# Loading weights and later chunks through eight row blocks with gaps, in a delta-rule attention and MoE kernel

## The chip, the cores and the metric

The kernel runs on one core of one Trainium2 chip. The metric is the device time of one execution in microseconds (us), taken as the median of several runs.

## What is computed

Two stages follow each other. The first is a delta-rule recurrence over 768 time steps for 4 x 8 heads of width 48; the second is a gated feed-forward layer (two products, multiplied, then a third) on the 3072 resulting rows.

```python
k_n = k / (np.linalg.norm(k, axis=-1, keepdims=True) + 1e-06)
for t in range(S):
    y[:, :, t] = einsum('bhd,bhde->bhe', q[:, :, t], state)
    v_old = einsum('bhde,bhd->bhe', state, kt)
    state = state + bt * einsum('bhd,bhe->bhde', kt, vt - v_old)
...
a = x @ w_a          # 384 -> 1536
b = x @ w_b
return a * b @ w_out # 1536 -> 384
```

The weights arrive as 64-bit floats, the rest as 32-bit floats.

## The kernel before

**Tiling.** The 768 steps are cut into 24 chunks of 32 (`NCH`), in six groups of four. For a group, `prep` squares keys and values for norms and multiplies the transposed keys and queries of each chunk with each other (`gram_mm`, 128 small matmuls of 32x64 for a whole group in sets of 32); `solve` inverts the triangular systems of the group on VectorE (DVE); `steps` walks its chunks in order, updates the state in PSUM (`S_ps`) and writes the chunk's result, transposed and split into two fp16 parts, to `xb`. Chunks share their input tiles in pairs: `kb` holds natural keys, `vnb` values, `rawb` transposed keys and queries, and `late` is one large tile that serves as weight staging, as one more place for those inputs, and as output buffer.

**Weights.** There are 12 weight blocks, each 1152 KB (128 rows of 1152 float64). `weights(p)` loads one into a slot (two slots in `late`, one in `wh`), unpacks it to float32 on DVE with one TENSOR_SCALAR and two SCALAR_TENSOR_TENSOR of 128x1152, takes its norm (ScalarE, ACT, square with a sum, then a matmul with `ones`), and splits it into a high and a low part (`wh`, `wo`). For the first four blocks the low part goes through TensorE (PE: `zit`, `neg1`, `negr` matmuls).

**MoE.** `moe` does for a pair of chunks and one weight block 18 fp16 matmuls of 128x256, two PSUM evacuations and 6 matmuls of 128x384. These make up most of the PE work (2592 and 864 matmuls).

**Loads.** All loads and stores are issued on SyncE's queue (SP) by `load` (line 690 and on). Some are held back by tiny GpSimd (POOL) copies into the target that read an earlier target (the list `NEXT`, and `prep` for groups 2 and up), so that a load starts when an earlier one has landed. The host pads rows of weights and of `kqt` by 64 bytes, so that each of 128 rows gives four pieces.

**The order.** Nothing is issued where it is written. The code records operations in `Plan`; `Plan.order` runs a list scheduler over the whole program (`pack`, 6 passes with changing priorities) and `Plan.issue` (line 471) writes the instructions per engine in the order found. `pack` has its own prices: 475 ns of SP time for a load plus bytes/400 ns of transfer (`op.move`), and in `fetch` a price for fetching PE's instructions. There PE's stream is cut into blocks of 256 words (two words for a matmul, four in fp32), a next block is asked for when the one before it is entered, and it comes 3500 ns later, or 5600 ns later while a load is under way by the plan (`LOADED`). An operation that would run out of fetched words is put off in favour of another. Where PE would wait in the first 60 us of the plan, `issue` puts in filler matmuls of `ones` (line 477, 128x256 fp32; they have no reader), up to `SHY` = 1500 ns before the awaited operation. An engine executes its instructions in the order written, so any change of a price can move all that comes after.

Of the kernel before, what the change touches and what calls it, by code (L numbers as in the profile page):

```python
# [15 lines left out]
I32 = mybir.dt.int32  # L16
# [10 lines left out]
P = 128  # L27
# [3 lines left out]
NFC = FF // P  # L31
# [29 lines left out]
class Plan:  # L61
# [131 lines left out]
    def add(self, eng, fn, name, args, kw):  # L193
        isap = lambda a: isinstance(a, bass.AP)
        outs = [a for a in args[:1]] + [kw[k] for k in ("accum_out",) if k in kw]
        ins = [a for a in list(args[1:]) + [v for k, v in kw.items() if k != "accum_out"] if hasattr(a, "tensor")]
        if self.open is not None and self.open and self.open[-1].eng == eng:
            op = self.open[-1]
        else:
            op = Op(eng)  # L200
            kind = self.stream + ("_pe" if self.stream == "moe" and eng == "PE" else "")
            op.pri = len(self.ops) - URGENCY.get(kind, URGENCY.get(kind.rstrip("0123456789"), 0))
            op.deps, self.behind = self.behind, set()
            self.ops.append(op)
            op.tag, op.stream = name, self.stream
            if self.open is not None:
                self.open.append(op)
        op.calls.append((fn, args, kw, dict(self.lease)))
        if eng == "SP":
            op.dur = 475.0  # L210
            n = mybir.dt.size(outs[0].dtype)
            for d in outs[0].shape:
                n *= d
            op.move = max(n / 400.0, 20.0)
        else:
            dur = self.price(eng, name, outs, ins, kw)
            op.dur += dur
            if eng == "PE":
                n = 1
                for d in outs[0].shape[1:]:  # L220
                    n *= d
                k, m, f = ins[0].shape[0] / 128, ins[0].shape[-1] / 128, ins[0].dtype == F32
                op.use += (1 + 3 * f) * n / 2.4 * m * (k + 1) / 2 + 5 * f
                op.words += 4 if ins[0].dtype == F32 else 2
                if min(ins[0].shape[0], ins[0].shape[-1]) <= 64:
                    if len(op.calls) == 1:
                        op.dur += self.SWITCH
                    op.cold += 2 * dur
                else:
                    op.cold += max(outs[0].shape[-1] if len(outs[0].shape) == 2 else 64, 48) / 1.2 * (4 if ins[0].dtype == F32 else 1)  # L230
        for regs, aps in ((op.wr, outs), (op.rd, ins)):
            for a in aps:
                g = self.region(a)
                if g is not None:
                    k = g[:3]
                    n = self.leased(a)
                    if n is not None:
                        op.banks.add(n)
                        k = (n,) + k[1:]
                    regs[k] = regs.get(k, 0) | g[3]  # L240
# [169 lines left out]
        return at, stop, done, max(stop), ({b: h[0] for b, h in held.items()}, fill)  # L410

    MOVE = (1200.0, 1300.0)
    LOADED = (3500.0, 5600.0)
    BEGIN, IDLE, SINCE, UNTIL = 63, (50.0, 440.0), 1200.0, 60e3
    SHY, KEEP, GAIN, HEAT = 1500.0, 0.41, 0.42, (3.0, 430.0)

    def fetch(self, t, n, took, pos, come, dma):
        slip, come, known = 0.0, come[:], len(come)
# [68 lines left out]


@with_exitstack
def tile_kernel(ctx, tc, kqt, kn, vn, begin, w, out):  # L490
    nc = tc.nc
    plan = Plan(nc)
    V, A, T, G, SP = (
        plan.engine(e, o)
        for e, o in (("DVE", nc.vector), ("ACT", nc.scalar), ("PE", nc.tensor), ("POOL", nc.gpsimd), ("SP", nc.sync))
    )
# [35 lines left out]
    WB = 2 * (6 * P + DM)  # L532
# [4 lines left out]
    slots = [late[:, 0:WB], late[:, WB : 2 * WB], whf[:, 3 * WB : 4 * WB]]  # L537
# [17 lines left out]
    def rawp(c):  # L555
        s = SLOT[c // 2]
        return rawb[:, 2 * s : 2 * s + 2] if s < 3 else lf[:, 0:2048].rearrange("p (c d) -> p c d", c=2)

    def knp(c):
        s = SLOT[c // 2]  # L560
        return knb[:, 2 * s : 2 * s + 2] if s < 3 else lf[:, 4352:5120].rearrange("p (c d) -> p c d", c=2)

    def vnp(c):
        s = SLOT[c // 2]
        return vnb[:, 2 * s : 2 * s + 2] if s < 3 else lf[:, 2816:3584].rearrange("p (c d) -> p c d", c=2)
# [117 lines left out]

    loaded, whole = set(), set()

    def target(c, what):
        t = {"w": lambda: slots[c].bitcast(F32), "k": lambda: knp(c)[:, 0], "v": lambda: vnp(c)[:, 0], "r": lambda: rawp(c)[:, 0], "r0": lambda: rawp(c)[:, 0], "r1": lambda: rawp(c)[:, 1]}
        return t[what]()[0:1, 0:1]

    def load(c, what):  # L690
        if (c, what) in loaded:
            return
        loaded.add((c, what))
        if what == "w":
            SP.dma_start(slots[c].rearrange("p (n d) -> p n d", n=4), w[c].bitcast(I32)[:, :, 0 : WB // 4])
        elif what == "k" and c == 0:
            SP.dma_start(kb[:, 0 : begin.shape[1]], begin)
        elif what == "k":
            SP.dma_start(knp(c).rearrange("p c d -> p (c d)"), kn[c // 2])
        elif what == "v":  # L700
            SP.dma_start(vnp(c).rearrange("p c d -> p (c d)"), vn[c // 2])
        elif what == "r":
            SP.dma_start(rawp(c).rearrange("p c (h d) -> p (c h) d", h=2), kqt[c // 2][:, :, 0:512])
        else:
            i = int(what[1])
            loaded.add((c, "r"))
            SP.dma_start(rawp(c)[:, i].rearrange("p (h d) -> p h d", h=2), kqt[c // 2][:, 2 * i : 2 * i + 2, 0:512])

    grams, rest = {}, []

# [40 lines left out]
    def prep(g):  # L751
        chs = GROUPS[g]
        ss = sst
        if g > 1:
            last = []
            for c in chs[2], chs[0]:
                for part in "k", "r0", "r1", "v":
                    if (c, part[0]) in loaded and part != "r1":
                        continue
                    if last:  # L760
                        G.tensor_copy(target(c, part), target(*last))
                    load(c, part)
                    last = c, part
# [426 lines left out]
def _layout(inputs):  # L1190
    f = lambda x: np.ascontiguousarray(x)
    q, k, v = (np.asarray(inputs[n]) for n in ("q", "k", "v"))
    beta = np.asarray(inputs["beta"])

    def tr(x):
        return x.reshape(B, 2, 2, 2, NCH, C, D)

    kq = np.stack([tr(k), tr(q)], axis=4)
    kq[:, :, :, 1] = kq[:, :, :, 1, ::-1].copy()
    kqt = kq.transpose(5, 3, 7, 0, 1, 2, 4, 6).reshape(NCH // 2, 2, 2, D, 1024).transpose(0, 2, 3, 1, 4)  # L1200
    gaps = np.zeros((NCH // 2, 2, 64, 2048), np.float32)
    gaps[:, :, 0:D] = kqt.reshape(NCH // 2, 2, D, 2048)
    pieces = np.zeros((NCH // 2, P, 4, 512 + 16), np.float32)
    pieces[..., 0:512] = gaps.reshape(NCH // 2, P, 4, 512)

    def natl(x):

        return x.reshape(B, 2, 4, NCH, C, D).transpose(3, 2, 4, 0, 1, 5).reshape(NCH // 2, 2, P, 384).transpose(0, 2, 1, 3).reshape(NCH // 2, P, 768)

    bn = beta.reshape(B, 2, 4, NCH, C).transpose(2, 4, 3, 0, 1).reshape(P, NCH, 8)  # L1210
    bp = np.zeros((P, NG, 4, 8), np.float32)
    for g, chs in enumerate(GROUPS):
        for i, c in enumerate(chs):
            bp[:, g, i] = bn[:, c]
    perm = np.empty(DM, np.int64)
    for j in range(3):
        for hp in range(4):
            for e in range(32):
                cc = j * 32 + e
                perm[j * 128 + hp * 32 + e] = ((cc // D) * 4 + (hp ^ 1)) * D + cc % D  # L1220

    masks = np.zeros((P, 32 + P + 2), np.float32)
    masks[:, 0:32] = np.tile(np.triu(np.ones((32, 32), np.float32), 1), (4, 1))
    masks[:, 32 : 32 + P] = np.eye(P, dtype=np.float32)
    masks[:, 32 + P :] = [[1 - p // 32 % 2, p // 32 % 2] for p in range(P)]
    wab = np.stack([np.asarray(inputs["moe_w_a"])[perm], np.asarray(inputs["moe_w_b"])[perm]])
    wab = wab.reshape(2, 3, P, NFC, P).transpose(3, 2, 0, 1, 4).reshape(NFC, P, 6 * P)
    w = np.concatenate([wab, np.asarray(inputs["moe_w_out"]).reshape(NFC, P, DM)], axis=2)
    wide = np.zeros((NFC, P, 4, 288 + 8), w.dtype)
    wide[..., 0:288] = w.reshape(NFC, P, 4, 288)  # L1230
    nat = f(natl(k))
    return {
        "kqt": pieces,
        "kn": nat,
        "vn": f(natl(v)),
        "first": f(np.concatenate([bp.reshape(P, NG * 32), masks, nat[0]], axis=1)),
        "w": wide.view(np.int64),
    }


# [15 lines left out]
```

## Time and profile before

| what | value |
|---|---|
| median of 3 runs | 656.53 us (655.1 to 660.78) |
| the profiled execution: its time | 658.43 us |
| its span, first to last instruction | 656.6 us, so 1.8 us lie around it |
| PE matmul busy | 625.9 us (95%) |
| DVE, ACT, POOL busy | 404.8, 270.4, 25.7 us |
| mean granted PE clock | 0.961 of full speed |
| DMA traffic | 42.78 MB, mean 65 GB/s |
| instruction packets, queue q8 | 95, 1.56 MB |
| weight load, issue to landing | 6.8 us median of the ten into `late` |

All instructions but the fillers carry one line, L486, since one statement issues them; groups are told apart by tiles. PE stands for matmuls, PEld for the weight load into the array that precedes each. A row of the timeline gives start, duration, engine, line, operation and in brackets the idle time before it with what ended it. "issue" there means that the engine waited for nothing that the profile records. PEclk is the granted share of PE's full clock; the DMA column is the busy share of the 16 DMA engines.

### The profile page before, as it was taken

How to read it: one execution, taken by the hardware profiler on the slowest of the kernel's cores; microseconds unless marked ns; L12 is line 12 of the kernel's file. 1: busy time of each engine (PE TensorE's matmuls, PEld its weight loads, DVE VectorE, ACT ScalarE, POOL GpSimd, SP SyncE). 2: the span in 40 equal slices, each digit the busy share in tenths (PEclk: the TensorE clock that was granted, in tenths of full speed). 3: DMA queues.
4: the chain of work that ended last, by engine and by line, in shares of the span. 5: the costliest groups of instructions: out<-in, count | busy, mean ns of one | idle time of the engine just before them, and what ended most of it. 6: DMA issues, size and time to landing. Idle time of an engine off the chain costs nothing.

```text
span 656.6 us, 26617 instructions
## 1 busy us (share of the span) xinstructions
PE 625.9 (95%) x12184; PEld 535.3 (82%) x12184; DVE 404.8 (62%) x1059; ACT 270.4 (41%) x599; POOL 25.7 (4%) x62
## 2 busy tenths in 40 slices
PE   7788999998999999999999999999999999999997
PEld 6575688777788887888878888888888888888887
DVE  5796699768666995448965389754686533222222
ACT  4245684245445634323373234733324333232322
POOL 0000000000012200000020000200000000000000
PEclk8858799879999999999999999999999999999999
DMA  7837202212276000004300033000000000000000
GB/s 252 312 130 272 80 4 74 80 70 76 70 226 190 19 2 27 4 14 134 108 2 29 4 115 112 26 4 28 3 1 26 4 3 25 1 25 2 25 1 24
DMA packets 19824, 42.78 MB, mean 65 GB/s; under 512 B 1280, under 2 KB 4352, under 8 KB 19712
## 3 DMA queue, kind: packets, MB, share of 16 engines
q1 hardware_dynamic: 19712, 41.08, 18.9%
q8 instruction: 95, 1.56, 1.0%
q14 instruction: 17, 0.14, 0.1%
HBM read 36.36 MB, written 4.72 MB: 63 GB/s over the span
## 4 chain that ended last, share of the span: by engine, by line
PE 78%; DVE 12%; ACT 4%; issue 3%; ACTq 0%
PE bank L486 75%; DVE b L486 3%; PE S_ps L486 3%; DVE tmp L486 2%; ACT sqf L486 2%; DVE wh L486 1%; DVE ghl L486 1%; DVE late L486 1%; DVE g L486 1%; ACT ghl L486 1%; ACT tt L486 1%; ACT a L486 0%; DVE sc L486 0%; DVE ss L486 0%; DVE s L486 0%
## 5 line engine op out<-in xcount | busy, mean ns | idle before, releaser
L486 PEld LDWEIGHTS <-wh 128*128 128x128 f16 x2592 | 241.2, 98 | 50.6 <-issue 22.4
L486 PE MATMUL bank<-xb,wh 128*128 128x256 f16 x2160 | 259.8, 273 | 2.2 <-issue 2.2
L486 PE MATMUL bank<-wo,ghl 128*128 128x384 f32 x864 | 192.3, 356 | 0.6 <-issue 0.6
L486 PEld LDWEIGHTS bank<-wo,ghl 128*128 128x128 f32 x864 | 145.2, 190 | 4.8 <-issue 1.6
L486 ACT COPY a<-bank 128x256 f32<-128x256 f32 x144 | 53.6, 372 | 195.4 <-PE bank L486 195.3
L486 DVE TENSOR_TENSOR g<-bank,a 128x256 f32<-128x256 f32 x144 | 60.8, 422 | 114.8 <-ACT a L486 113.5
L486 DVE TENSOR_TENSOR ghl<-g,ghl 128x256 fp32r<-128x256 f32 x144 | 62.3, 432 | 35.0 <-ACT ghl L486 33.8
L486 ACT CAST ghl<-g 128x256 fp32r<-128x256 f32 x144 | 58.1, 404 | 60.4 <-DVE g L486 59.6
L486 PE MATMUL bank<-late,wh 128*128 128x256 f16 x432 | 52.0, 273 | 1.2 <-ACT u L486 1.2
L486 DVE TENSOR_TENSOR b<-b,tmp 128x31 f32<-128x31 f32 (+20 forms) x154 | 50.9, 330 | 2.8
L486 DVE TENSOR_TENSOR tmp<-b,b 128x31 f32<-128x31 f32 (+20 forms) x154 | 50.8, 330 | 2.9
L486 ACT ACTIVATE y<-bank,sc 128x384 f32<-128x384 f32 x24 | 14.0, 582 | 45.1 <-PE bank L486 42.8
L486 DVE SCALAR_TENSOR_TENSOR y<-bank,sc,y 128x384 f32<-128x384 f32 x23 | 14.2, 616 | 29.6 <-ACT y L486 29.6
L486 PEld LDWEIGHTS bank<-rawb 48*32 48x32 f32 x1280 | 21.2, 117 | 7.7 <-issue 3.7
L486 PE MATMUL bank<-rawb 48*32 48x64 f32 x1280 | 24.0, 232 | 3.3 <-DMA rawb<-in_kqt 3.3
L486 DVE TENSOR_TENSOR b<-bank,dc 128x256 f32<-128x256 f32 x24 | 14.5, 605 | 20.6 <-PE bank L486 17.1
L486 PEld LDWEIGHTS bank<-sh,rawb 48*64 48x64 f32 x1216 | 21.3, 144 | 6.7 <-issue 5.3
L486 PEld LDWEIGHTS bank<-f,tt 32*32 32x32 f32 x1472 | 17.9, 107 | 9.3 <-issue 5.5
L486 PE MATMUL bank<-sh,rawb 48*64 48x48 f32 x1216 | 23.9, 229 | 0.7 <-issue 0.7
L486 PE MATMUL bank<-u,at 32*32 32x48 f32 x1536 | 22.3, 206 | 1.9 <-issue 1.9
L486 PE MATMUL bank<-f,tt 32*32 32x48 f32 x1472 | 21.2, 206 | 2.5 <-issue 1.4
L486 DVE TENSOR_TENSOR f<-vnb,bank 128x384 f32<-128x384 f32 x38 | 19.9, 548 | 5.7 <-PE bank L486 5.1
(120 smaller groups left out, 552.8 us busy)
## 6 DMA issues: line engine op xcount, KB each, us to landing
late<-in_w SPq DMA_DIRECT2D x10, 1152.0 KB, 6.8
rawb<-in_kqt SPq DMA_DIRECT2D x12, 512.0 KB, 3.7
out<-late SPq DMA_DIRECT2D x24, 192.0 KB, 1.9
rawb<-in_kqt SPq DMA_DIRECT2D x4, 1024.0 KB, 7.0
vnb<-in_vn SPq DMA_DIRECT2D x10, 384.0 KB, 3.2
kb<-in_kn SPq DMA_DIRECT2D x9, 384.0 KB, 3.9
wh<-in_w SPq DMA_DIRECT2D x2, 1152.0 KB, 9.7
late<-in_kqt SPq DMA_DIRECT2D x4, 512.0 KB, 3.7
```

The costliest lines, as they stand in the source:

```text
L486: fn(*(self.place(a, lease) for a in args), **{k: self.place(a, lease) for k, a in kw.items()})
```

## The change

`load` no longer reads 128 rows. The host cuts each array into 8 blocks of 16 rows, with 2048 bytes of padding behind each block, and `eight` builds a source pattern whose outermost dimension is 8 (block), then 16 or 64 pieces within the block, then the piece. The bytes moved and their places in SBUF are as before. This holds for the 12 weight blocks and for keys, values and `kqt` of chunk 4 and on; the first two pairs of chunks have arrays of their own (`kqt0`, `kn0`, `vn0`) that are read by 128 rows as before. The two halves `r0` and `r1` of a `kqt` load become one load of 1024 KB, which makes eight loads and eight gates fewer. The planner's prices change with it: 200 bytes per ns for loads of eight rows, 3700 ns in place of 5600 for a fetch beside a load, and fillers up to 500 ns before the awaited operation.

```diff
-            op.move = max(n / 400.0, 20.0)
+            op.move = max(n / (200.0 if ins[0].shape[0] == 8 else 400.0), 20.0)
...
-    LOADED = (3500.0, 5600.0)
+    LOADED = (3500.0, 3700.0)
...
-    SHY, KEEP, GAIN, HEAT = 1500.0, 0.41, 0.42, (3.0, 430.0)
+    SHY, KEEP, GAIN, HEAT = 500.0, 0.41, 0.42, (3.0, 430.0)
...
+    def eight(src, n, d):
+        return bass.AP(src.tensor, src.offset, [[src.shape[1], 8], [(src.shape[1] - 512) // n, n], [1, d]])
...
-            SP.dma_start(slots[c].rearrange("p (n d) -> p n d", n=4), w[c].bitcast(I32)[:, :, 0 : WB // 4])
+            SP.dma_start(slots[c].rearrange("p (n d) -> p n d", n=4), eight(w[c].bitcast(I32), 64, WB // 4))
...
-            SP.dma_start(knp(c).rearrange("p c d -> p (c d)"), kn[c // 2])
+            SP.dma_start(knp(c).rearrange("p c d -> p (c d)"), kn0[c // 2] if c < 4 else eight(kn[c // 2], 16, 768))
...
-            SP.dma_start(vnp(c).rearrange("p c d -> p (c d)"), vn[c // 2])
+            SP.dma_start(vnp(c).rearrange("p c d -> p (c d)"), vn0[c // 2] if c < 4 else eight(vn[c // 2], 16, 768))
...
-            SP.dma_start(rawp(c).rearrange("p c (h d) -> p (c h) d", h=2), kqt[c // 2][:, :, 0:512])
-        else:
-            i = int(what[1])
-            loaded.add((c, "r"))
-            SP.dma_start(rawp(c)[:, i].rearrange("p (h d) -> p h d", h=2), kqt[c // 2][:, 2 * i : 2 * i + 2, 0:512])
+            SP.dma_start(rawp(c).rearrange("p c (h d) -> p (c h) d", h=2), kqt0[c // 2][:, :, 0:512] if c < 4 else eight(kqt[c // 2], 64, 512))
...
-                for part in "k", "r0", "r1", "v":
-                    if (c, part[0]) in loaded and part != "r1":
+                for part in "k", "r", "v":
+                    if (c, part) in loaded:
...
+    def blocks(x):
+        x = x.reshape(len(x), 8, -1)
+        return f(np.concatenate([x, np.zeros((len(x), 8, 2048 // x.itemsize), x.dtype)], axis=2))
```

Since the prices change, the order of nearly the whole program changes. Two places matter below. The first is ScalarE's order in the first 21 us. The four `tt` rows copy the four Gram results of the first group out of PSUM; the `sqf` rows are squares of values and of `rawb` for norms.

```order
 L486 COPY tt_86<-bank_62 128x256
 L486 ACTIVATE sqf,sc_127<-vnb 128x768
-L486 ACTIVATE sqf,sc_127<-rawb 48x1024
 L486 COPY tt_87<-bank_63 128x256
-L486 ACTIVATE sqf,sc_127<-rawb 48x1024
-L486 ACTIVATE sqf,sc_127<-vnb 128x768
 L486 ACTIVATE sqf,sc_127<-rawb 48x1024
 L486 COPY tt_88<-bank_64 128x256
 L486 ACTIVATE sqf,sc_127<-rawb 48x1024
+L486 ACTIVATE sqf,sc_127<-vnb 128x768
+L486 ACTIVATE sqf,sc_127<-rawb 48x1024 x2
```

The third copy now has one square ahead of it instead of two, and the fourth has two instead of five; three squares moved behind the fourth copy.

The second place is the head of PE's order: fillers (`ones`), the first group's Gram matmuls (`rawb`, 32 for a chunk), then the first matmuls that need the solved systems (`b_3_71`).

```order
-L477 MATMUL bank_66<-ones 128x256 x6
+L477 MATMUL bank_66<-ones 128x256 x7
 L486 MATMUL bank_61<-rawb 32x64 x32
 L486 MATMUL bank_62<-rawb 32x64 x32
+L477 MATMUL bank_66<-ones 128x256
 L486 MATMUL bank_63<-rawb 32x64 x32
 L486 MATMUL bank_64<-rawb 32x64 x32
-L477 MATMUL bank_66<-ones 128x256 x20
+L477 MATMUL bank_66<-ones 128x256 x26
 L486 MATMUL bank_65<-b_3_71,tt_85 32x16 x32
 L486 MATMUL bank_61<-b_3_71,tt_86 32x16 x32
```

There are 34 fillers instead of 26: one more ahead of the first Gram, one between the second and the third, six more behind the fourth.

More of the change, by code (lines that the diff above doesn't have):

```diff
@@ L489, in tile_kernel @@
 @with_exitstack
-def tile_kernel(ctx, tc, kqt, kn, vn, begin, w, out):
+def tile_kernel(ctx, tc, kqt0, kn0, vn0, begin, kqt, kn, vn, w, out):
     nc = tc.nc
@@ L1230, in _layout @@
     wide[..., 0:288] = w.reshape(NFC, P, 4, 288)
-    nat = f(natl(k))
+    nat, vat = natl(k), natl(v)
+    def blocks(x):
+        x = x.reshape(len(x), 8, -1)
+        return f(np.concatenate([x, np.zeros((len(x), 8, 2048 // x.itemsize), x.dtype)], axis=2))
     return {
-        "kqt": pieces,
-        "kn": nat,
-        "vn": f(natl(v)),
+        "kqt0": f(pieces[0:2]),
+        "kn0": f(nat[0:2]),
+        "vn0": f(vat[0:2]),
         "first": f(np.concatenate([bp.reshape(P, NG * 32), masks, nat[0]], axis=1)),
-        "w": wide.view(np.int64),
+        "kqt": blocks(pieces),
+        "kn": blocks(nat),
+        "vn": blocks(vat),
+        "w": blocks(wide.view(np.int64).reshape(NFC, P, -1)),
     }
```

## The prediction

> **What bounds the kernel now.** I read the page first, then the waits of PE, then the stretches around PE's longest waits, and last the chain of the first 48 us.
>
> ```profile
> PE 625.9 (95%) x12184; PEld 535.3 (82%) x12184; DVE 404.8 (62%) x1059; ACT 270.4 (41%) x599; POOL 25.7 (4%) x62
> PEclk8858799879999999999999999999999999999999
> PE 78%; DVE 12%; ACT 4%; issue 3%; ACTq 0%
> ```
>
> PE is busy for 95% of the span and carries 78% of the chain that ended last. The number of useful matmuls stays the same, so only three things can shorten the span: time in which PE waits, time in which its granted clock is low (the first third of PEclk), and the prologue ahead of PE's steady work. PE's waits in total, longest first:
>
> ```profile
> PE bank L486 <- issue: 12.1, 11, 2.5
> PE bank L486 <- DVE b L486: 4.6, 1, 4.6
> ```
>
> The largest is "issue": 12.1 us in 11 pieces in which nothing that the profile records was late. The timeline has them one by one:
>
> ```profile
> 66.78 0.34 PE L486 MATMUL bank<-wh,neg 128*128 128x384 f16 x1 [2.54 <-issue]
> 102.00 0.26 PE L486 MATMUL bank<-sh,rawb 48*64 48x48 f32 x2 [0.40 <-issue]
> 121.70 0.24 PE L486 MATMUL bank<-b,tt 32*32 32x16 f32 x3 [1.38 <-issue]
> 135.00 1.03 PE L486 MATMUL bank<-f,tt 32*32 32x48 f32 x41 [1.35 <-issue]
> 155.19 0.70 PE L486 MATMUL bank<-xb,wh 128*128 128x256 f16 x5 [1.65 <-issue]
> 171.84 0.28 PE L486 MATMUL bank<-u,at 32*32 32x48 f32 x7 [0.75 <-issue]
> 259.29 0.28 PE L486 MATMUL bank<-u,at 32*32 32x48 f32 x5 [1.19 <-issue]
> ```
>
> Stretches just before such waits (columns: start:end, length, busy time of each engine, PEclk, DMA share, GB/s):
>
> ```profile
> 61.20:64.20 3.00, 2.85 (x132) 2.08 (x132) 3.00 (x6) 1.10 (x2) 0.00 (x0) 1.00 0.94 360
> 117.70:120.30 2.60, 2.60 (x132) 2.00 (x131) 2.60 (x5) 0.96 (x3) 0.00 (x0) 1.00 0.02 6
> 130.60:133.60 3.00, 2.74 (x91) 1.75 (x92) 0.98 (x6) 2.20 (x5) 0.00 (x0) 0.88 1.03 376
> 150.50:153.50 3.00, 3.00 (x107) 2.62 (x96) 3.00 (x6) 2.03 (x6) 0.00 (x0) 1.00 0.77 298
> 255.50:258.10 2.60, 2.60 (x187) 2.32 (x180) 1.28 (x3) 0.31 (x1) 0.00 (x0) 1.00 0.02 6
> ```
>
> There are two kinds. Before 120.3 and 258.1 the DMA engines are idle and PE runs well over a hundred matmuls in under 3 us: it uses up its instructions faster than they come. Before 64.2, 133.6 and 153.5 the DMA engines are full with a load. How the instructions came is in the DMA view, ahead of and after 152.7 us:
>
> ```profile
> q1 hardware_dynamic: 416, 0.94, 99.4%
> q14 instruction: 2, 0.02, 2.1%
> ...
> q8 instruction: 1, 0.02, 5.3%
> q1 hardware_dynamic: 11, 0.00, 0.9%
> ```
>
> From 150.3 to 152.7 queue q1, the load, holds 99.4% of the engines and q8 moves nothing. From 152.7 to 154 the load has ended and one packet of q8 passes; it takes 5.3% of 16 engines over 1.3 us, or 1.1 us of one engine, and PE resumes at 155.19. So the packet of instructions ran when the load was out of the way. I take q8 to be PE's instruction fetch, and the load to be what holds it up.
>
> **What the change removes.** If a load uses eight of the 16 engines and the fetch is carried by another, a fetch beside a load costs what a quiet one costs. The three waits beside loads are 2.54 + 1.35 + 1.65 = 5.54 us, 1.85 on average. The four quiet ones above (0.40, 1.38, 0.75, 1.19) average 0.93. The low end is that each of the three becomes a quiet wait: 3 x 0.92 = 2.8 us gained. The high end is that all go: 5.5 us. I take the middle, **4.2 us**. The other waits on fetches stay, though perhaps elsewhere.
>
> The clock follows such gaps:
>
> ```profile
> 64.20:66.80 2.60, 0.07 (x6) 0.02 (x2) 1.76 (x4) 0.68 (x2) 0.00 (x0) 1.00 0.74 182
> 68.00:75.00 7.00, 6.86 (x72) 3.93 (x72) 5.33 (x10) 4.08 (x9) 0.00 (x0) 0.51 0.27 104
> 133.00:139.70 6.70, 5.35 (x140) 4.64 (x140) 2.19 (x7) 2.39 (x5) 0.00 (x0) 0.50 0.19 72
> ```
>
> After 2.6 us with 0.07 us of work, PE runs 7 us at half clock; around the wait at 133.65 us it is another 6.7 us. At full clock the 6.86 and 5.35 us of busy time would be half as long, if all of it is bound by the clock: at most 3.4 + 2.7 = 6.1 us. At least nothing is gained, since a shorter gap may still drop the clock, and the second drop begins 0.65 us before its wait. I take **2.5 us**, about two fifths.
>
> **What it moves.** In the first group the chain runs through ScalarE:
>
> ```profile
> 15.88 0.35 ACT L486 COPY tt<-bank 128x256 f32<-128x256 f32 x1
> 17.48 0.84 ACT L486 ACTIVATE sqf<-vnb 128x768 bf16<-128x768 f32 x1
> 18.44 1.06 ACT L486 ACTIVATE sqf<-rawb 48x1024 bf16<-48x1024 f32 x1
> 19.50 0.35 ACT L486 COPY tt<-bank 128x256 f32<-128x256 f32 x1
> 19.88 0.61 DVE L486 TENSOR_TENSOR b<-bank,dc 128x256 f32<-128x256 f32 x1 [3.20 <-ACT tt L486]
> 16.50 10.34 PEld L477 LDWEIGHTS bank<-ones 128*128 128x128 f32 x40 [0.17 <-issue]
> 16.50 10.74 PE L477 MATMUL bank<-ones 128*128 128x256 f32 x40
> 31.87 1.91 PE L486 MATMUL bank<-b,tt 32*32 32x16 f32 x128 [4.64 <-DVE b L486]
> ```
>
> DVE waits 3.20 us for the fourth `tt` copy, then solves the group and releases PE at 31.87. In the new order the fourth copy has only squares ahead of it that end by about 17 us, and the fourth Gram result is there at about 16.9 (16.5 before, plus about half a filler of 0.9 us, since the new filler falls into a wait for `rawb`). So the copy starts near 17.1 instead of 19.50, and DVE could release PE 2.4 us earlier, at 29.5. The fillers then matter: 20 took 10.74 us, an average of 0.54; six more at that price, started at 16.9, end at 30.9, and at 0.44 (an estimate of the full-clock price, if the first four of the 20 took 0.9 each, the two-rate fit to 10.74) at 30.2. PE can thus start the solved group between 29.5 and 30.9. I take 30.0, a gain of **1.9 us**, with 1.0 and 2.4 as ends. The filler ahead of the first Gram lies in the wait for `rawb`, and costs nothing.
>
> The later order of PE, DVE and ACT is rearranged throughout. No row prices that. Its work is the same; its bounds are the quiet waits that it can add or avoid, about one of 0.93 us each way for every few moved, so plus or minus 3 us. I take 0.
>
> **What it adds.** Loads get slower.
>
> ```profile
> 16.00:30.00 14.00, 11.23 (x63) 9.17 (x53) 9.55 (x31) 4.86 (x10) 0.71 (x4) 0.85 0.95 352
> late<-in_w SPq DMA_DIRECT2D x1, 1152.0 KB, 5.4
> 42.01 1.81 SPq L486 DMA_DIRECT2D late<-in_w  x2
> 46.74 0.54 SPq L486 DMA_DIRECT2D wh<-in_w  x1
> 55.73 0.75 DVE L486 TENSOR_SCALAR wh<-late 128x1152 int32<-128x1152 int32 x1
> 61.16 0.75 DVE L486 TENSOR_SCALAR wh<-late 128x1152 int32<-128x1152 int32 x1
> 70.03 0.75 DVE L486 TENSOR_SCALAR late<-wh 128x1152 int32<-128x1152 int32 x1
> ```
>
> In a full stretch 352 GB/s at a share of 0.95 is 23.2 GB/s per engine, so eight move 185. A block of 1.18 MB takes 3.2 us on 16 and 6.4 on eight. Alone it landed after 5.4 us (the one issued at 126.2); now after 8.6. The tightest place is the train of three issued from 42.0 us: landing at 50.6, then 6.4 apart, 57.0 and 63.4. DVE first reads them at 55.73, 61.16 and 70.03, with 5.1, 4.2 and 6.6 us to spare; the train and its readers shift together with the prologue. Cost nothing. Without that cover, the most is a train that holds DVE back by a whole transfer, 3.2 us. Fewer gates and loads on POOL and SP cost and bring nothing: neither is on the chain.
>
> [...]
>
> **The sum.** 4.2 + 2.5 + 1.9 = 8.6 us from the profiled execution's 658.43 us (span 656.6) gives 649.8. That execution is 1.9 above the median of 656.53; against the median the sum is 647.9, and I predict **648.0 us**.
>
> **Rivals.**
> (a) The fetch waits for memory or for the queue as such, not for an engine: then freeing engines does nothing. For it: the fetch packets in the trace show only when they ran, not where. Against: q8 ran as soon as q1 was done. Only the prologue gains: 656.5 - 1.9 = 654.6 us.
> [...]
> (b) The gain is made and given back: new dense runs of small matmuls end at block limits, with five or six more quiet waits of 0.93 us. For it: 7 of the 11 issue waits are not beside a full load, and the new plan moves everything. 648 + 5 = 653 us.
> (c) Slower: the engine that carries q8 is among the eight. Its place is every load, whose time on that engine doubles, so that twice as many fetches meet one. Six waits of 1.85 instead of three add 5.5 us; the clock drops after three more at 1.7 us each (half of a 3.4 us stretch), 5.1; less the prologue's 1.9: 656.5 + 8.7 = 665.2 us. It decides from the moment that q8's packets still start only when q1 ends. For it: the trace does not say which engine q8 uses, and eight of 16 is even odds. Against: the view by queue shows q8 only where q1 is out of the way, and never how the engines share; and fewer fetches than I assume may meet a load, since the twelve weight blocks are the only long ones, which would leave the time near (a).
>
> **How the numbers follow.** The forecast gets 0.47, and within it the time lies from 643 to 651: all of the 5.5 and most of the 6.1 at one end, 2.8 without clock at the other. Rival (b) gets 0.17, (a) 0.16, (c) 0.20. A measurement of this kernel tells about 1% from no change, 6.6 us, so "faster" is below 650.0. Of the forecast's 0.47, 0.42 lies below; of (b) 0.03 and of (a) 0.01: 0.46. "Slower" is above 663.1: 0.11 of (c), the rest of it being spread down to (a), and 0.01 of (b): 0.12. The rest is 0.42. The range from 642 to 660 leaves out most of (c) and the ends of the forecast.
>
> **What would show it.** Right: the loads' GB/s fall to about 185 in full stretches at a DMA share near 0.5; q8 packets pass in the middle of loads; no "issue" wait beside a load is over about 1 us; the fourth `tt` copy starts near 17 us and the solved group near 30; PEclk loses one or two of its low stretches between 60 and 140 us. Wrong: a share near 1 during loads, q8 still at their end, PE waiting for `late` or `wh` by way of DVE between 50 and 80 us, or issue waits that sum to 12 us again.

## The result: 690.63 us, slower by 5.4%

| | before | after |
|---|---|---|
| median | 656.62 us (4 runs, 655.1 to 660.78) | 690.63 us (4 runs, 689.51 to 697.62) |
| the profiled execution: time, span | 658.43, 656.6 us | 690.89, 689.1 us |
| mean granted PE clock | 0.961 | 0.948 |

The ratio is 1.0537, with a 95% interval of 1.0496 to 1.0579. The forecast was 648.0 us, with a range up to 660; the time lies 30 us above that range and beyond the slower rival's 665.2 too.

The page of the changed kernel (busy time of PE, its granted clock in 40 slices, the chain that ended last):

```profile
PE 637.9 (93%) x12200; PEld 542.3 (79%) x12200; DVE 401.3 (58%) x1059; ACT 270.3 (39%) x599; POOL 25.1 (4%) x54
PEclk8956999999999699999998999998999999999999
PE 60%; DMA 26%; DVE 7%; ACT 3%; issue 3%; POOL 1%; SPq 0%; POOLq 0%; ACTq 0%
```

Before, DMA had no share in the chain; now it has 26%. PE is busy 12 us longer (637.9 against 625.9) for the same matmuls and eight fillers more, at a lower mean clock. What PE waited for, in total, times and longest:

```profile
PE bank L486 <- issue: 11.9, 10, 2.2
PE bank L486 <- ACT tt L486: 9.6, 3, 4.6
PE bank L486 <- DMA rawb<-in_kqt: 8.4, 2, 6.1
PE bank L486 <- ACT sqf L486: 4.8, 2, 3.4
```

"issue", the wait that was to shrink, is where it was (12.1 before). Three others have grown under it: a load itself (3.3 before), and two steps of ScalarE (1.4 and 0.9 before). The two longest of `tt`, 4.6 us each, come behind loads of `vnb` that land at 371.7 and 461.1 us: from there the chain runs through ScalarE to PE at 373.28 and 464.13. Stretches inside weight loads (start:end, length, busy time of PE, PEld, DVE, ACT, POOL, then clock, DMA share, GB/s), the first two beside the first and a later block, the third a wait of PE within a load, the last what follows it:

```profile
15.00:24.00 9.00, 9.00 (x118) 8.06 (x111) 7.36 (x22) 6.05 (x12) 0.17 (x1) 0.94 0.52 121
128.00:137.00 9.00, 8.33 (x237) 6.59 (x236) 4.67 (x14) 3.85 (x9) 0.00 (x0) 1.00 0.52 125
138.40:140.60 2.20, 0.01 (x2) 0.01 (x2) 1.46 (x4) 0.60 (x1) 0.00 (x0) 1.00 0.51 123
140.60:146.00 5.40, 5.40 (x117) 3.91 (x117) 4.32 (x6) 3.68 (x9) 0.00 (x0) 0.68 0.52 122
```

The share of 0.52 is that of eight busy engines out of 16, as the forecast took it ("near 0.5"); which engines they are, the profile does not say. But the loads move 121 to 125 GB/s and not 185: 125 / (16 x 0.52) is 15 GB/s per busy engine, where the full stretch before gave 23.2 (352 GB/s at a share of 0.95). Single instructions from the timeline of the same kernel (start, duration, idle time before it and what ended it):

```profile
16.83 0.60 DVE L486 TENSOR_TENSOR b<-bank,dc 128x256 f32<-128x256 f32 x1 [0.41 <-PE bank L486]
17.82 0.35 ACT L486 COPY tt<-bank 128x256 f32<-128x256 f32 x1
28.80 1.29 PE L486 MATMUL bank<-b,tt 32*32 32x16 f32 x128 [0.63 <-DVE b L486]
62.88 0.76 DVE L486 TENSOR_SCALAR wh<-late 128x1152 int32<-128x1152 int32 x1 [7.47 <-DMA late<-in_w]
140.59 0.45 PE L486 MATMUL bank<-b,tt 32*32 32x16 f32 x33 [2.23 <-issue]
231.92 1.96 PE L486 MATMUL bank<-sh,rawb 48*64 48x48 f32 x64 [6.12 <-DMA rawb<-in_kqt]
```

The head of the program did better than forecast: the fourth `tt` copy starts at 17.82, DVE's product of the fourth Gram result (`b<-bank,dc`) even ahead of it at 16.83 (19.88 before), and the solved group at 28.80 (31.87 before). Then the loads hold DVE up by 7.47 us at 62.88, and PE by 6.12 us at 231.92. The second of these lies in a stretch that the chain gives to loads alone (start, duration, what):

```profile
189.50 12.05 DMA late<-in_kqt
201.87 10.82 DMA late<-in_vn
213.09 6.09 DMA kb<-in_kn
219.50 12.29 DMA rawb<-in_kqt
232.10 10.20 DMA vnb<-in_vn
```

These are the loads of one group, each held back by a gate until the one before it has landed. Five of them take 51 us in a row. The same 80 us of both kernels, first of before:

```profile
180.00:260.00 80.00, 78.64 (x1215) 69.13 (x1204) 59.19 (x170) 38.30 (x86) 10.76 (x22) 1.00 0.32 97
```

and of after:

```profile
180.00:260.00 80.00, 69.48 (x1014) 59.85 (x1013) 42.91 (x122) 31.98 (x72) 7.92 (x18) 0.91 0.39 103
```

Before, PE was busy for 78.64 of the 80 us at full clock; now for 69.48, at 0.91. Loads fill the chain again at 326 to 372 and 434 to 461 us. PE loses less there: it is busy for 42.33 of the 46 and 25.51 of the 27 us.

### The profile page after: what moved, and what is told of

It reads as the page before. It is cut to its first block, busy times and chain, and to the rows that moved or that the text cites. A ratio compares the mean times of both kernels' runs of the same rounds, so it can differ in the third digit from the quotient of the medians.

```text
span 689.1 us, 26606 instructions
## 1 busy us (share of the span) xinstructions
PE 637.9 (93%) x12200; PEld 542.3 (79%) x12200; DVE 401.3 (58%) x1059; ACT 270.3 (39%) x599; POOL 25.1 (4%) x54
## 4 chain that ended last, share of the span: by engine, by line
PE 60%; DMA 26%; DVE 7%; ACT 3%; issue 3%; POOL 1%; SPq 0%; POOLq 0%; ACTq 0%
PE bank L486 57%; DMA rawb<-in_kqt 6%; DMA vnb<-in_vn 4%; DMA wh<-in_w 4%; DMA late<-in_kqt 3%; DMA kb<-in_kn 3%; PE S_ps L486 3%; DMA late<-in_w 2%; DMA late<-in_vn 2%; DVE b L486 2%; DVE tmp L486 1%; DVE g L486 1%; DMA late<-in_kn 1%; DVE ghl L486 1%; ACT sqf L486 1%
## 5 line engine op out<-in xcount | busy, mean ns | idle before, releaser
L486 PEld LDWEIGHTS <-wh 128*128 128x128 f16 x2592 | 243.7, 99 | 53.5 <-issue 23.0
L486 PE MATMUL bank<-xb,wh 128*128 128x256 f16 x2160 | 263.9, 276 | 2.6 <-DVE g L486 1.4
L486 PE MATMUL bank<-wo,ghl 128*128 128x384 f32 x864 | 194.5, 358 | 3.4 <-ACT ghl L486 2.6
L486 DVE TENSOR_TENSOR b<-b,tmp 128x31 f32<-128x31 f32 (+20 forms) x154 | 50.9, 331 | 2.6
L486 PE MATMUL bank<-f,tt 32*32 32x48 f32 x1472 | 23.4, 213 | 13.2 <-ACT tt L486 9.6
L486 PEld LDWEIGHTS bank<-f,tt 32*32 32x32 f32 x1472 | 19.5, 112 | 20.2 <-ACT tt L486 10.8
L486 PEld LDWEIGHTS bank<-sh,rawb 48*64 48x64 f32 x1216 | 21.0, 144 | 10.8 <-issue 8.9
L486 PE MATMUL bank<-u,at 32*32 32x48 f32 x1536 | 23.8, 209 | 5.2 <-issue 5.1
L486 PEld LDWEIGHTS bank<-u,at 32*32 32x32 f32 x1536 | 19.7, 110 | 8.9 <-issue 7.6
L486 PEld LDWEIGHTS S_ps<-u,kb 32*48 32x48 f32 x1216 | 17.1, 127 | 5.5 <-issue 4.3
```

The lines of the kernel that those rows point to most:

```text
L486: fn(*(self.place(a, lease) for a in args), **{k: self.place(a, lease) for k, a in kw.items()})
```

## The experiments

Four questions: is the loss in the loads or in the new order; why are the loads slow; does a fetch beside a load on eight engines come sooner; and what is the rest of the order worth. Times are medians. The kernel before stood at 655.91 us beside e1 to e4, at 654.4 beside e5 to e8 and at 655.33 beside e9 to e12. A ratio is that to the kernel before, with its 95% interval.

**e1_rows128: the new order, loads by 128 rows.** The price stays as the change has it, so every engine's order is that of the change.

```diff
-            op.move = max(n / (200.0 if ins[0].shape[0] == 8 else 400.0), 20.0)
+            op.move = max(n / (200.0 if ins[0].tensor.name in ("in_kqt", "in_kn", "in_vn", "in_w") else 400.0), 20.0)
...
-            SP.dma_start(slots[c].rearrange("p (n d) -> p n d", n=4), eight(w[c].bitcast(I32), 64, WB // 4))
+            SP.dma_start(slots[c].rearrange("p (n d) -> p n d", n=4), w[c].bitcast(I32)[:, :, 0 : WB // 4])
```

(and in the same way for `kn`, `vn` and `kqt`).

> The changed kernel with every instruction in the same order on every engine, but each load reading 128 rows as before the change. Theory A (the loss comes from the loads: 121 GB/s in the stretch from 15 to 24 us, 125 from 128 to 137 us, where before 377 and 364 stood): about 655 us, between 648 and 662, with waits on instruction fetches beside loads as before. Theory B (the loss lies in the new order and its prices): 680 us or more, since nothing of the order is taken back. Weight loads should move 350 GB/s or more again under both.

Measured: 651.03 us, ratio 0.993 (0.9907 to 0.9953). From 41 to 55 us the DMA moves 342 GB/s again, at a share of 0.90. The loads alone thus cost 1.0537 / 0.993, or 6.1%: about 40 us. The new order by itself gains 0.7%, some 5 us. From the timeline of this kernel (the profiled execution was its slowest, 655.99 us):

```profile
17.03 11.49 PE L477 MATMUL bank<-ones 128*128 128x256 f32 x52
29.16 1.03 PE L486 MATMUL bank<-b,tt 32*32 32x16 f32 x99 [0.64 <-DVE b L486]
160.50 0.38 PE L486 MATMUL bank<-u,at 32*32 32x48 f32 x8 [3.15 <-issue]
```

The solved group starts 2.7 us earlier than before. The wait of 3.15 us at 160.50 is new, and will matter below.

**e2_loads8: the order of before, loads by eight blocks.** Prices, fillers and gates as before; the halves of `kqt` are kept and stored apart, so that each can be read in eight blocks.

```diff
-            SP.dma_start(slots[c].rearrange("p (n d) -> p n d", n=4), w[c].bitcast(I32)[:, :, 0 : WB // 4])
+            SP.dma_start(slots[c].rearrange("p (n d) -> p n d", n=4), eight(w[c].bitcast(I32), 64, WB // 4))
...
-            SP.dma_start(rawp(c)[:, i].rearrange("p (h d) -> p h d", h=2), kqt[c // 2][:, 2 * i : 2 * i + 2, 0:512])
+            SP.dma_start(rawp(c)[:, i].rearrange("p (h d) -> p h d", h=2), eight(kqth[c // 2 * 2 + i], 32, 512))
```

> The kernel before with its own order, untouched on every engine, but weights and later chunks read in eight row blocks with gaps (halves of kqt stay halves). Theory A: the slow loads alone cost time, 670 to 700 us; a weight block takes about 10 us instead of 3 to 4. Theory B: 650 to 658 us, since the order of before had room for slower loads (4 to 6 us at the train of 42 us). If fetches are freed, the 1.35 and 1.65 us waits near 134 and 154 us go under both.

Measured: 717.78 us, ratio 1.0946 (1.0872 to 1.102). PE's waits in it:

```profile
PE bank L486 <- DVE g L486: 18.1, 7, 5.1
PE bank L486 <- DMA rawb<-in_kqth: 10.9, 1, 10.9
...
PE bank L486 <- issue: 8.0, 10, 1.7
...
PE S_ps L486 <- issue: 3.7, 4, 2.9
```

Put into an order that does not know of them, the slow loads cost 62 us, and one load holds PE for 10.9 us at a stretch. The change's plan as a whole, its prologue with it, took 27 of these back (690.63 us). The waits on fetches sum to 11.7 us in these two rows, against 13.7 before (12.1 and 1.6). This need not be a gain of the loads: PE waits longer elsewhere in this run (18.1 us for DVE's `g` alone), and may therefore need its instructions later, which was not shown. As expected, the wait of 1.35 us ahead of `f,tt` fell to 0.26 and that of 1.65 us is gone from its place; so is that of 2.54. But two others came, 1.72 us up to 148.43 beside a slow load and 2.90 us up to 156.54 at the end of one: the waits moved more than they shrank.

**e3_loads: the loads alone.** One weight block after another, each in another cut; only stores of zeros run beside the first 3 us of some. A new kernel; its transfers:

```diff
+    for n in range(2):
+        rows128(n)
+    for n in range(2):
+        cut(view["b"], n, 1, 8, 16, 512)
...
+        cut(view["c"], n, 4, 8, 4, 512)
+    for n in range(2):
+        cut(view["d"], n, 2, 8, 8, 512)
+    for n in range(2):
+        cut(view["d"], n, 1, 16, 8, 512)
...
```

(`cut`: transfers per block, blocks per transfer, rows per block, padding).

> Leaves out the whole computation: loads of weight blocks alone, each waiting for the one before, two of each kind in this order: 128 rows; 8 blocks of 16 rows (four times); four transfers of 32 rows as 8 blocks of 4; two transfers of 64 rows as 8 blocks of 8; 16 blocks of 8 rows; 8 blocks of 16 again. Zeros are stored. [...] Theory A2 (an engine is slower per se when only eight carry a load, or the gaps in memory slow the reads): four of 8x4 no faster than 8x16, and 16x8 about twice 8x16 (A2 by engine count) . Theory A3 (compute beside the loads slows them): 8x16 near 185 here.

Measured, in stretches of (in this order) 128 rows, 8 blocks of 16 rows twice, four transfers of 8 blocks of 4 rows twice ("quarters"), two of 8 blocks of 8, and 16 blocks of 8. The last three columns are clock, DMA share and GB/s:

```profile
4.00:7.00 3.00, 0.00 (x0) 0.00 (x0) 1.00 0.93 267
19.00:26.40 7.40, 0.00 (x0) 0.00 (x0) 1.00 0.52 116
31.50:38.40 6.90, 0.00 (x0) 0.00 (x0) 1.00 0.52 125
67.00:72.00 5.00, 0.00 (x0) 0.00 (x0) 1.00 0.51 198
73.00:78.00 5.00, 0.00 (x0) 0.00 (x0) 1.00 0.52 205
80.00:88.00 8.00, 0.00 (x0) 0.00 (x0) 1.00 0.52 143
103.00:106.00 3.00, 0.00 (x0) 0.00 (x0) 1.00 1.02 228
```

The slowness is there with no compute beside the loads: 116 to 125 GB/s. And it isn't the number of engines: quarters also fill half of them (share 0.51, 0.52) and move 198 to 205, which is 205 / (16 x 0.52) = 24.6 GB/s per busy engine, what the prediction took for granted. That speaks against the first half of theory A2 (quarters no faster than 8 blocks of 16); its second half, 16 blocks of 8 at about twice their pace, came out (228 against 116 to 125). Theory A3 is out: it had 185 here for 8 blocks of 16. Rows 8 apart in SBUF lie between, at 143 (two transfers of 8 blocks of 8). 128 rows moved 267 GB/s, with stores beside them. A whole block took 9.9 to 10.8 us in eight blocks, 5.9 to 6.5 in quarters and 5.1 to 5.3 in 128 rows.

**e4_quarters: the change with its loads in quarters.** Each load is four transfers of 32 rows, each of 8 blocks of 4 rows; order and bytes are those of the change.

```diff
-            op.move = max(n / (200.0 if ins[0].shape[0] == 8 else 400.0), 20.0)
+            op.move = max(n / (50.0 if ins[0].shape[0] == 8 else 400.0), 20.0)
...
+    def quarters(dst, src, n, d):
+        with plan.group():
+            for i in range(4):
+                SP.dma_start(dst[32 * i : 32 * i + 32], bass.AP(src.tensor, src.offset + 8 * i * src.shape[1], [[src.shape[1], 8], [4 * (src.shape[1] - 512) // n, n // 4], [1, d]]))
```

> The changed kernel with the same order, but each load of eight blocks of 16 rows cut into four transfers of 32 rows, each in 8 blocks of 4 rows, so that still eight engines carry it while the rows written at one time are 4 apart. [...] Theory A2: loads near 120 GB/s and 685 to 695 us. Theory B: 680 us or more. In any case SP issues three more transfers a load, about 0.4 us each, off the path.

Measured: 653.87 us, ratio 0.9965 (0.9934 to 0.9996). Nearly all of the 40 us is back, with eight engines as in the change: from 14 to 24 us the DMA moves 193 GB/s at a share of 0.53. The interval meets that of e1_rows128, so loads at half the share, at this pace, cost little or nothing against those by 128 rows in this order. Its waits on fetches:

```profile
PE bank L486 <- issue: 15.6, 11, 3.4
```

With 0.4 us ahead of `S_ps` it is 16.0, and not less than the 15.0 (14.1 and 0.9) of e1_rows128, which has the same order and fills all 16 engines. So with loads at the pace that the prediction assumed, freeing eight engines still shortens the waits on fetches by nothing that the total shows.

**e5_sides: memory or SBUF.** The loads alone again. `cross` reads rows 16 apart in memory into rows 4 apart in SBUF, `near` reads blocks 4 rows apart in memory into rows 16 apart in SBUF; then 8 blocks of 16 as in the change, and eight transfers of 8 blocks of 2 rows.

```diff
+    def cross(n):
+        x, pitch = view["b"], 16 * ROW + 512
+        for i in range(4):
+            o = x.offset + n * 8 * pitch + i * 4 * ROW
+            nc.sync.dma_start(late[32 * i : 32 * i + 32], bass.AP(x.tensor, o, [[pitch, 8], [STEP, 16], [1, PIECE]]))
+
+    def near(n):
+        x, pitch = view["c"], 4 * ROW + 512
+        nc.sync.dma_start(late, bass.AP(x.tensor, x.offset + n * 32 * pitch, [[pitch, 8], [STEP, 64], [1, PIECE]]))
```

> Leaves out the whole computation: weight blocks loaded alone, one after the other, two of each kind: four transfers of 32 rows as 8 blocks of 4 rows (181 and 199 GB/s in the run before); the same four, but read from places 16 rows apart in memory; 8 blocks of 16 rows into SBUF rows 16 apart, but read from places 4 rows apart; 8 blocks of 16 rows on both sides (110 to 120); eight transfers of 16 rows as 8 blocks of 2; four of 8x4 again. [...] Theory A2 (it is the places in memory that are read at the same time): 180, about 115, about 180, 115, 180, 180.

Measured, in the order `cross`, `near` twice, blocks of 2 rows:

```profile
15.00:20.00 5.00, 0.00 (x0) 0.00 (x0) 1.00 0.52 205
31.00:38.00 7.00, 0.00 (x0) 0.00 (x0) 1.00 0.52 116
43.00:51.00 8.00, 0.00 (x0) 0.00 (x0) 1.00 0.52 117
81.00:86.00 5.00, 0.00 (x0) 0.00 (x0) 1.00 0.52 145
```

The memory side made no difference in these cuts: read with the change's pitch, but written 4 rows apart, a load moves 205 GB/s; read from close by and written 16 rows apart, it moves 116. What is left is the spacing of the rows in SBUF, 4 against 16; which engine writes a row, and so which rows are written at the same time, the trace does not record. Quarters also put four transfers into the queue where the change puts one. That is not what makes them quick: they land one after the other, 1.4 us apart in the steady part, and 288 KB in 1.44 us is again 205 GB/s for one transfer; eight transfers (blocks of 2) are slower than four. Theory A2 had `cross` and `near` the other way round (about 115 and about 180), and blocks of 2 rows at 180, where the two loads of that kind moved 141 and 187 GB/s.

Why 8 blocks of 8 rows (143 GB/s) and blocks of 2 rows (141 and 187) lie between the two paces, and what in the write makes rows 16 apart slow, is open.

**e6_shy: before, with the later fillers alone.**

```diff
-    SHY, KEEP, GAIN, HEAT = 1500.0, 0.41, 0.42, (3.0, 430.0)
+    SHY, KEEP, GAIN, HEAT = 500.0, 0.41, 0.42, (3.0, 430.0)
```

> The kernel before with one number changed, fillers up to 500 ns before the awaited operation instead of 1500; loads, prices of loads and fetches as before. The plan comes out another: 31 instead of 26 fillers, and the fourth copy out of PSUM stays behind five squares on ScalarE. If the gain of the new order (651.0 against 655.9 us) is the prologue on ScalarE, 655 to 657; if it is the fillers, about 652.

Measured: 647.89 us, ratio 0.9897 (0.988 to 0.9914). One number of the planner gives at least as much as the whole new order of e1_rows128. It was more than either side had expected.

**e7_true: loads by 128 rows, the merged halves, the true prices.** As the change, but with `n / 400.0`, `LOADED` of 5600 and loads as in e1_rows128.

```diff
-    LOADED = (3500.0, 3700.0)
+    LOADED = (3500.0, 5600.0)
```

> The loads by 128 rows with the merged halves, planned at the prices that fit them (400 bytes per ns, 5600 ns for a fetch beside a load), fillers up to 500 ns before. If the plan gains by knowing what its loads cost, 648 to 651 us, below the 651.0 of the order made for slow loads; if the gain was the luck of one order, 652 to 657.

Measured: 648.26 us, ratio 0.99 (0.9884 to 0.9915), like e6_shy. It lies in the first range, but e6_shy, with true prices and the old halves, does as well: merging the halves and dropping eight gates adds nothing that can be measured. Against e1_rows128 the intervals meet (0.9907 to 0.9953 there).

**e8_fill20: e1_rows128 with 20 fillers behind the fourth Gram, not 26.** Nothing else moves.

```diff
-                    for _ in range(n):
+                    for _ in range(20 if n == 26 else n):
```

> The changed kernel's order with loads of 128 rows, with 20 instead of 26 fillers behind the fourth Gram, nothing else moved. If the fillers' warmth counts: the stretch at half clock that begins at 33.7 us begins a window of 3.4 us earlier and may last longer, 652 to 655 us. If only the order counts: 650 to 652, and PE waits 3 us longer ahead of the solved group at 29 us, which is unchanged.

Measured: 642.7 us, ratio 0.9821 (0.9801 to 0.9842), the fastest so far and well below what either side had expected. Six matmuls without a reader cost 1.1%, or 7 us.

**e9_words: the six fillers back as 12 small ones.** 20 large fillers and 12 of 32x32 in bfloat16. By the planner's count (four words for a matmul in fp32, two for one in bfloat16) they are as long as 26 large ones, and they hold next to no work.

```diff
-                for k, n in enumerate(self.fill.get(i, ())):
+                for k, n in enumerate([12, 20] if self.fill.get(i) == [0, 26] else self.fill.get(i, ())):
```

> The order of the change with loads of 128 rows; behind the fourth Gram 12 small bf16 fillers of 32x32 and 20 large ones, in place of 26 large ones. Each large one is four instructions on PE and each small one two, so that the number of instructions ahead of all that follows is the same as with 26 (651.0 us), and the time filled nearly that with 20 (642.7). Theory L (six fillers cost 8 us because they shift where the instruction blocks of all later work begin): 649 to 653 us. Theory W (they cost it by the work and the clock of the first 35 us): 641 to 645.

Measured: 651.62 us, ratio 0.9939 (0.9911 to 0.9967). The time is that of e1_rows128, though PE's work is that of e8_fill20. So what costs is the number of instructions ahead of the rest, and not their work. The traces show what it shifts. A wait near 46 us breaks one group of `sh,rawb` matmuls in all of these kernels. The number behind the last x is what was left of the group after the wait, in e1_rows128, e9_words and e8_fill20:

```profile
45.63 1.02 PE L486 MATMUL bank<-sh,rawb 48*64 48x48 f32 x52 [0.37 <-issue]
45.41 1.02 PE L486 MATMUL bank<-sh,rawb 48*64 48x48 f32 x52 [0.33 <-issue]
46.55 0.80 PE L486 MATMUL bank<-sh,rawb 48*64 48x48 f32 x40 [0.86 <-issue]
```

A large filler gives two matmul records (26 are x52 in the row at 17.03), a small one gives one. Six fillers fewer, and the wait comes 12 records later; 12 small ones in their place, and it is back where it was. So this wait lies at a fixed count of instructions, and the fillers decide which of the later work it meets. e1_rows128 has its longest wait on a fetch, 3.15 us, at 160.50 (above). The same place in e9_words:

```profile
157.66 0.39 PE L486 MATMUL bank<-u,at 32*32 32x48 f32 x8 [3.12 <-issue]
```

and the waits over 2 us in e8_fill20:

```profile
64.84 0.33 PE L486 MATMUL bank<-sh,rawb 48*64 48x48 f32 x8 [2.19 <-issue]
153.99 1.81 PE L486 MATMUL bank<-sh,rawb 48*64 48x48 f32 x63 [2.17 <-issue]
```

The wait of 3.1 us ahead of `u,at` is gone without the six fillers, and comes back with the 12 small ones. The clock follows. Of e1_rows128:

```profile
50.00:75.00 25.00, 19.34 (x435) 13.12 (x439) 10.46 (x19) 9.09 (x20) 0.00 (x0) 0.73 0.40 138
120.00:170.00 50.00, 45.24 (x1341) 36.42 (x1341) 37.97 (x76) 23.76 (x53) 0.00 (x0) 0.93 0.29 98
```

and of e8_fill20:

```profile
50.00:75.00 25.00, 21.35 (x636) 14.93 (x635) 15.64 (x31) 14.48 (x30) 0.00 (x0) 0.93 0.47 164
120.00:170.00 50.00, 47.55 (x1374) 39.53 (x1373) 40.44 (x87) 26.36 (x55) 0.00 (x0) 0.97 0.29 101
```

From 50 to 75 us the clock is 0.93 where it was 0.73, and 636 matmul records pass where 435 did. e9_words stands between them there (0.80, 515 records) and at the clock of e1_rows128 from 120 to 170 (0.93). Which single wait decides is not settled.

**e10_quarters20: e4_quarters with 20 fillers.** The edit of e8_fill20 on e4_quarters.

```diff
-                    for _ in range(n):
+                    for _ in range(20 if n == 26 else n):
```

> The change with each eight-block load cut into four transfers of 32 rows, and 20 instead of 26 fillers behind the fourth Gram; order as in the change. Beside it stands the same with loads of 128 rows, 642.7 us. If eight engines left free spare PE its waits on instructions beside loads (about 6 us of such waits stand there at 51, 63 and 152 us): 637 to 641. If fetches that meet a load still wait often enough, or the slower loads take back what is gained: 642 to 650.

Measured: 652.59 us, ratio 0.9952 (0.9929 to 0.9975). Against e8_fill20 the intervals lie apart, by 1.3% or 8.6 us: in the better order, loads in quarters lose to loads by 128 rows. Its waits of PE:

```profile
PE bank L486 <- issue: 10.8, 11, 2.2
PE bank L486 <- DMA rawb<-in_kqt: 4.9, 2, 3.0
PE S_ps L486 <- issue: 4.1, 3, 2.7
```

Waits on fetches sum to 14.9 us here (two rows), against 11.5 in e8_fill20. So the freed engines are no help to fetches in this order either, and PE waits 4.9 us for loads (3.3 in e8_fill20). From 170 to 270 us PE is busy for 96.31 us at a clock of 0.97, and in e8_fill20 for 99.25 at 1.00. How the 8.6 us divide between slower loads, four issues on SP instead of one, and fetches was not isolated.

**e11_fill23 and e12_fill14: other counts.** e1_rows128 with 23 and with 14 fillers in place of 26.

```diff
-                    for _ in range(n):
+                    for _ in range(23 if n == 26 else n):
```

> As the order of the change with loads of 128 rows, 23 fillers behind the fourth Gram (26: 651.0, 20: 642.7). Theory W: between the two, 645 to 649. Theory L: anywhere from 640 to 655, with no reason to lie between.

> As the order of the change with loads of 128 rows, 14 fillers behind the fourth Gram. Theory W (fewer fillers, less work in the way): below 642, unless the clock falls for lack of them. Theory L: anywhere from 640 to 655.

Measured: 648.2 us, ratio 0.9876 (0.9848 to 0.9905), and 644.22 us, ratio 0.9802 (0.977 to 0.9835). With 26, 23, 20 and 14 fillers the ratio is 0.993, 0.9876, 0.9821 and 0.9802; the last two cannot be told apart. Fewer is better down to 20, and no more from there to 14. Taken alone, 23 fillers fall where theory W put them and 14 do not; it is e9_words that tells the theories apart. In the group near 46 us, 46 records are left with 23 fillers and 28 with 14, again two for each filler. The two fastest versions, e8_fill20 and e12_fill14, load by 128 rows.

## Why the prediction was wrong

**The step that failed** is in "What it adds": "In a full stretch 352 GB/s at a share of 0.95 is 23.2 GB/s per engine, so eight move 185. A block of 1.18 MB takes 3.2 us on 16 and 6.4 on eight", and then "Cost nothing". It took the pace of an engine to be the same in every cut. e3_loads and e5_sides show 116 to 125 GB/s for this cut, and 198 to 205 at the same DMA share (0.51 and 0.52) for rows 4 apart in SBUF. That eight blocks take eight engines was an assumption of the forecast; what the runs show of it is the share, 0.52 in the changed loads against 0.95 in a full stretch before. A block takes 9.9 to 10.8 us alone. With that pace the train of three blocks, issued from 46.4 us in the changed kernel, could not be covered: DVE waited 7.47 us for a block of it. e4_quarters shows that the rest of the step held: at the pace that it assumed, the loads cost at most a few us in this order (in that of e10_quarters20, up to the 8.6 us that were not divided).

**The second fault of that step** is what it left out. It weighed one train of three weight blocks and called it the tightest. The loads of the later groups, held one behind the other by gates, were not priced; five in a row take 51 us of the chain after 189 us, and more follow twice. e1_rows128 puts the whole price of the loads at about 40 us, a term that stood in the sum as zero with a bound of 3.2.

**"What the change removes", 4.2 us, gained nothing.** Its premise, that a load holds the packet of instructions up until it ends, was read off one of the three waits, the one at 152.7. The kernel before already shows otherwise at another of them: in its DMA view from 132.6 to 134 us, just ahead of the wait that ends at 135.00, a q8 packet passes while the load fills most of the 16 engines (packets, MB, share):

```profile
q1 hardware_dynamic: 224, 0.50, 91.7%
q8 instruction: 1, 0.02, 4.4%
```

So that q8 passes in the middle of a load in the changed kernel, as here between 15 and 24 us, is no gain of the change:

```profile
q1 hardware_dynamic: 466, 1.07, 50.9%
q8 instruction: 1, 0.02, 0.9%
```

That q8 feeds PE, the prediction's other assumption, is borne out: at all 24 waits of 0.3 us and more on "issue" in the two kernels, PE resumes 1.25 to 1.61 us after a q8 packet has ended. But PE still waits: 2.23 us ahead of 140.59, with the load at a share of 0.51, and the next q8 packet comes only at 146.00. The forecast said that no wait beside a load would be over about 1 us. With the waits ahead of `S_ps` the sum was 13.7 us before and is 12.7 now; in the pairs with one order, 16 engines against eight, it is 15.0 and 16.0, 11.5 and 14.9. So the load was not, or not alone, what held these fetches up, or eight engines leave that unchanged. Which engine carries q8 is still open. The list of waits was also not whole: it held seven of the 11 pieces, and with the four that it left out (1.38, 0.55, 0.60, 0.31) the quiet waits average 0.82 us and not 0.93.

**The clock, 2.5 us,** went the other way. In the profiled executions (1 - mean clock) x span was 25.6 us before and 35.8 after, with new gaps at the waits on loads. In e1_rows128 it is 20.3, which is 5.3 less and within the 0 to 6.1 given, but not by the cause given: the waits on fetches that it was to follow from are 15.0 us there, against 13.7 before. The 3.4 us of half clock that rival (c) counts with stand in the kernel before, from 122.70 to 126.10 us (clock 0.50):

```profile
122.70:126.10 3.40, 3.40 (x72) 2.60 (x71) 3.40 (x4) 0.37 (x1) 0.00 (x0) 0.50 0.03 5
```

**The prologue, 1.9 us,** had the right sign, by luck in part: the solved group started at 28.80 and in e1_rows128 at 29.16 (30.0 forecast, 29.5 as the early end), a gain of 2.7 to 3.1 us, above the 1.0 to 2.4 given. The copy that was to release DVE did start earlier, at 17.82 (17.1 forecast), 1.7 us ahead of before. But DVE did not wait for it: its product of the fourth Gram result started at 16.83, released by PE, where before it waited 3.20 us for the copy and started at 19.88. These 3.05 us, and not the copy's 1.7, are what the group gained. The 26 fillers lasted 11.49 us (the row at 17.03 above), hardly more than 20 before (10.74), where the step gave six more 2.6 to 3.2 us.

**The re-ordering, 0 with 3 either way,** was mis-sized. Six fillers move the time by 1.1%, 7 us, and e9_words shows that it isn't by the work that they hold but by their number of instructions. The prediction asked whether the fillers end before they are needed, and never what their instructions shift.

**The rivals.** (a) had the total of the fetches right; its 654.6 us took the loads as free, too. (b) gave the gain back in more waits on fetches, whose sum did not grow. (c) had the right sign by the wrong cause: q8 packets passed before q1 had ended (132.6 to 134 us before, 15 to 24 us now), and the waits on fetches did not grow. None of the three priced a slow load, though the text had two of its own signs of being wrong come true: "PE waiting for `late` or `wh` by way of DVE between 50 and 80 us" (DVE 7.47 us at 62.88, then PE 2.94 us for DVE at 65.38), and waits on "issue" that sum to 12 us again.

## What to carry to other kernels

Before a transfer is cut for fewer engines, run that load alone in the cut that is planned, and in another that spaces the rows in SBUF differently: the count of engines gave 185 GB/s, this cut moves 116 to 125 and quarters 198 to 205. When a planner's price is changed together with what it prices, run each alone; here the order hid 27 us of a loss of 62. Where PE's stream is short of instructions, try a few counts of fillers as a change of its own: here 26, 23, 20 and 14 gave ratios from 0.993 to 0.9802 in one order.

## What the runs showed of the hardware

- Loads of 1152 KB at a DMA share of 0.51 to 0.52 moved 116 to 125 GB/s cut into 8 blocks 16 rows apart in SBUF, and 198 to 205 cut into blocks 4 rows apart (e3_loads, e5_sides); with the pitches in memory exchanged they moved 116 and 205 (e5_sides).
- 24 more instructions (by the plan's count) ahead of the program, with almost no work in them, took the ratio from 0.9821 to 0.9939, 1.2% or some 8 us; the wait on a fetch near 46 us came 12 matmul records later for six fillers fewer (e8_fill20), and was back with 12 small ones in their place (e9_words).
- A q8 packet can run in the middle of a load that takes 91.7% of the 16 engines' time (before, 132.6 to 134 us) as of one that takes 50.9% (after, 15 to 24 us), and PE can still wait 2.23 us beside a load at a share of 0.51 (after, up to 140.59 us).
- A wait of some 2 us on PE can be followed by a low clock: 2.23 us, then 0.68 over 5.4 us in the changed kernel; 2.17 us up to 153.99 in e8_fill20, after which nine `xb,wh` matmuls took 2.06 us at 155.73. It need not be: after 2.41 us up to 63.74 in e4_quarters, 18 of them took 2.14 us at 65.15.
